# Feature tiles that overlap in the middle instead of doubled last columns, in a fused S5 scan and gated unit

## The chip, the cores and the metric

The kernel runs on one core of a Trainium2 chip. The metric is device time in microseconds of one launch, the median of the runs shown. The core has five engines, each with its own instruction stream that is worked off in order: TensorE (PE; its weight loads are shown apart as PEld), VectorE (DVE), ScalarE (ACT), GpSimd (POOL) and SyncE (SP). SP issues nearly all transfers here, and sixteen DMA engines carry them.

## The reference

x has 2048 tokens of 448 features. It is normalised over the features, and two branches read the result: a diagonal complex recurrence over time (S5), and a gated unit with inner width 1792. The output is `x + s * g`.

```
xn = layernorm(x)
Lam_bar = exp(dt * Lam);  Bu = xn @ B_bar.T          # 448 complex states
h[t] = Lam_bar * h[t-1] + Bu[t]                      # over 2048 tokens
s = 2 * Re(h @ C.T) + xn * Dskip
g = silu((sigmoid(xn @ w_gate) * (xn @ w_up)) @ w_down)
out = x + s * g                                      # bf16
```

## The kernel before

**Chunks.** The tokens are worked in four chunks of 512 (`TC`), each of four tiles of 128. All products with xn sum over features, so xn is turned: `xnT[c]` holds features on the partitions. 448 is three and a half times 128. The turned xn has four tiles: features 0 to 127, 128 to 255, 256 to 383, and a fourth in which features 384 to 447 lie twice, on partitions 0 to 63 and again on 64 to 127. For that the 64 last columns of the normalised xn are copied behind the 448 before the turn (`ln_twice`, and in chunk 0 `ln_turn`), so that a row has 512 columns. Chunk 0 is turned by TensorE through PSUM (`tps`, emptied by `ln_out`), chunks 1 to 3 by DMA transposes on the SP queue, one for each tile of 128 tokens.

**Two halves at a time.** Most products are issued as pairs on 64 partitions: one on the upper, one on the lower half of the array, side by side (`beside_each`, `Sum.add`, line 510). A sum over 448 features is seven such half products. The doubled fourth tile is what lets gate take its last 64 features from the upper half and up from the lower one: the weight rows 384 to 447 of gate and up lie together in `wt`, gate on partitions 0 to 63 and up on 64 to 127, the other rows in `wg` and `wu` as three tiles of 128.

**B and C.** B (448 x 448, real and imaginary) is loaded into `raw["b_re"]` and `raw["b_im"]`, the last columns are doubled (`emit_b_twice`, a memset for the real part), and eight DMA transposes from SBUF write `bT` (`emit_b`, line 297). C is loaded into `c_re` (room `raw_c`) and `c_im` (room `raw_re`, which `b_re` had before), with the doubled columns loaded as small extra DMAs, and is turned by eight DMA transposes (`emit_c_turn`, line 169) into `tc_re` and `tc_im`. Then `emit_c` makes seven scaled tiles `ct`: ScalarE writes a scratch tile, VectorE adds the other part. The scratch tiles take rooms that are free by then; `c_room` lists them, and the first pair lies in `raw_im`, where `b_im` had been.

**The order of the work** is written out: `keep_order` ties each engine's instructions to the written order. SP's order is: x of chunk 0, the weights of the first 512 inner columns, B, the weights of columns 512 to 1023, x of chunk 1, the first block of B turned, the last 768 weight columns around the second turn, Dskip, four more turns of B, x of chunk 2, then (`second_chunk`, and the calls of `at(0, 7, ...)`) two turns of xn, the last block of B, two more turns of xn, w_down, C, and with chunk 1 the turns of C. The tile framework gives each DMA one of eight semaphores in turn, so a DMA can only be issued when the eighth before it has landed.

In a chunk, `emit_line` names the pairs of units: a unit of the gate and up products (`gu_unit`, 128 inner columns) or of B (`bu_unit`, a block of states). For chunk 1 it begins (0, -1), (1, -2), then the down products of chunk 0 (`emit_downs`), then (2, 3), (4, -3), where -1 to -4 are B's blocks. Each product has a PSUM bank, and the eight banks are handed out in turn (`bank`). ScalarE empties the banks of gate, up, B and down; VectorE does the rotation, the scan and the gates. Between them `fill` and `at` place the other work: the first three C scalings stand on ScalarE after the second quarter of chunk 0's down products (`"down1"`).

Of the kernel before, what the change touches and what calls it, by code (L numbers as in the profile page):

```python
# [17 lines left out]
D = 448  # L18
# [9 lines left out]
CP = D // KT  # L28
NT = S_TOK // P
NPK = 2 * D  # L30
EPS = 1e-5
TWO_PI = 2.0 * math.pi
HALF_PI = 0.5 * math.pi
# [30 lines left out]
def kernel(  # L64
# [48 lines left out]
    skip = w.tile([P, D], BF16, name="skip")  # L113


    def load_rows(eng, t, mat, f0, f1):
        eng.dma_start(out=t[:, 0:3, f0:f1], in_=mat[0:384, f0:f1].rearrange("(kt p) f -> p kt f", p=P))
        eng.dma_start(out=t[0:64, 3, f0:f1], in_=mat[384:448, f0:f1])

    def load_w(eng, f0, f1, between=None):  # L120
        for t, mat in ((wg, B_w_gate), (wu, B_w_up)):
            eng.dma_start(out=t[:, :, f0:f1], in_=mat[0:384, f0:f1].rearrange("(kt p) f -> p kt f", p=P))
        if between:
            between()
        for mat, p0 in ((B_w_gate, 0), (B_w_up, 64)):
            eng.dma_start(out=wt[p0:p0 + 64, f0:f1], in_=mat[384:448, f0:f1])

    pool.memset(ident[:], 0.0)
    pool.affine_select(out=ident[:], in_=ident[:], compare_op=ALU.not_equal, fill=1.0, base=0,  # L129
# [126 lines left out]

    def ln_norm(c, j):
        t = c * TPC + j
        xb = xn[c % 3]
        if c < 2:  # L260
            dve.tensor_scalar(out=xb[:, j, 0:D], in0=x_t[c][:, j, :], scalar1=mv[:, t, 0:1],
                              scalar2=rsd[:, t, :], op0=ALU.subtract, op1=ALU.mult)
        else:
            act.activation(xb[:, j, 0:D], x_t[c][:, j, :], ACT.Identity, bias=nmr[:, t, :],
                           scale=rsd[:, t, :])

    def ln_turn(c, j):
        xb, cols = xn[c % 3], slice(j * P, (j + 1) * P)
        if c > 0:
            sync.dma_start_transpose(out=xnT[c][:, 0:KT, cols], in_=xb[:, j, :])  # L270
            return
        (dve if j < 2 else pool).tensor_copy(out=xb[:, j, D:DP], in_=xb[:, j, 384:D])
        for kt in range(KT):
            pe.transpose(tps[j % 2][:, kt, :], xb[:, j, kt * P:(kt + 1) * P], ident[:])  # L274

    def ln_twice(c, copy, j0=0, j1=TPC):
        copy(out=xn[c % 3][:, j0:j1, D:DP], in_=xn[c % 3][:, j0:j1, 384:D])
# [8 lines left out]
    def emit_b_twice():  # L286
        t = raw["b_im"]
        act.copy(out=t[:, 0:3, D:DP], in_=t[:, 0:3, 384:D])
        act.copy(out=t[0:64, 3, D:DP], in_=t[0:64, 3, 384:D])

    def emit_b(cc, pt):
        n = P if pt < 3 else 64
        if cc == 0:
            p0 = pt * P
        else:
            p0 = D if pt == 3 else 512 + pt * P
        sync.dma_start_transpose(out=bT[:, :, p0:p0 + n], in_=raw[("b_re", "b_im")[cc]][0:n, pt, :])

    def bu_cols(pt, cc):
        if pt == 3:  # L300
# [156 lines left out]
    def emit_c(i):  # L457
        pt = i // 2
        tre, tim = ctr["c_re"][:, pt, :], ctr["c_im"][:, pt, :]
        if pt == 3:  # L460
            ta, sa, tb, sb = tre, K["cr3"][:, 0:1], tim, K["nci2"][:, 3:4]
        elif i % 2 == 0:
            ta, sa, tb, sb = tre, K["cr2"][:, pt:pt + 1], tim, K["nci2"][:, pt:pt + 1]
        else:
            ta, sa, tb, sb = tim, K["ncr2"][:, pt:pt + 1], tre, K["nci2"][:, pt:pt + 1]

        if not c_room:
            for nm in ("raw_im", "raw_c"):
                both = []
                c_room.extend((nm, both, k) for k in range(2))  # L470
                if nm == "raw_im":
                    c_room.extend((None, None, None) for _ in range(2))
            c_room.append((None, None, None))
        nm, both, k = c_room[len(mixed)]
        mixed.append(i)
        if nm is None:
            tmp = sp.tile([P, D], FP32, name="c_tmp", tag="ctmp")[:]
        else:
            if k == 0:
                both.append(w.tile([P, 2, D], FP32, name="c_tmps", tag=nm))  # L480
            tmp = both[0][:, k, :]
        act.activation(tmp, tb, ACT.Copy, scale=sb)
        return lambda: dve.scalar_tensor_tensor(out=ct[:, i, :], in0=ta, scalar=sa, in1=tmp, op0=ALU.mult, op1=ALU.add)
# [207 lines left out]

    def gu_halves(c, ft, gt, ut, first, n0=0, n1=TC):
        f0, f1 = ft * P, (ft + 1) * P
        for t, p0 in ((gt, 0), (ut, 64)):
            pe.matmul(t[:, n0:n1], lhsT=wt[p0:p0 + 64, f0:f1],  # L695
                      rhs=xnT[c][p0:p0 + 64, 3, n0:n1], start=first, stop=not first)

    def gu_wholes(c, ft, gt, ut, first, n0=0, n1=TC, which=(0, 1)):
        f0, f1 = ft * P, (ft + 1) * P
        for t, wm in [((gt, wg), (ut, wu))[i] for i in which]:  # L700
            for kt in range(3):
                pe.matmul(t[:, n0:n1], lhsT=wm[:, kt, f0:f1], rhs=xnT[c][:, kt, n0:n1],  # L702
                          start=(first and kt == 0), stop=(not first and kt == 2))


    def gu_out(ft, gt, ub):
# [11 lines left out]
    def gu_unit(c, ft):  # L718
# [70 lines left out]

    def y_ops(c, j, rows, d0=0, d1=D, skipped=False):  # L790
        sl = slice(j * P, (j + 1) * P)
        o = [(ident[rows, :], xn[c % 3][rows, j, d0:d1], d0, d1)] if skipped else []
# [20 lines left out]

    def emit_two(c, j):

        xb, two = xn[c % 3][:, j:TPC:2, 0:D], slice(j, TPC, 2)
# [10 lines left out]

    def emit_rest_of(c, j):
        t = op_.tile([P, D], BF16, name="t_g", tag="zb", bufs=4)
        dve.tensor_tensor(out=t[:], in0=xn[c % 3][:, j, 0:D], in1=gs[c][:, j, :], op=ALU.mult)  # L830
# [64 lines left out]
    def ln_plan(c):  # L895
# [16 lines left out]
        at(own, "down0", 0.0, lambda: ln_twice(c, act.copy))  # L912

    dummy = w.tile([P, 1], FP32, name="dummy")
    act.activation(dummy[:], hpi[:], ACT.Exp)
# [86 lines left out]
    for t in (TPC, TPC + 2):  # L1002
# [13 lines left out]
    def second_chunk(j0):  # L1016
        ln_pow(TPC + j0, 2)
        for j in (j0, j0 + 1):
            ln_norm(1, j)
        ln_twice(1, dve.tensor_copy, j0, j0 + 2)  # L1020
# [4 lines left out]
    at(0, 7, 0.0, lambda: sync.dma_start(out=wd[:], in_=B_w_down.rearrange("(ft p) d -> p ft d", p=P)))  # L1025
    at(0, 7, 0.0, lambda: load_c("c_re", A_C_re, A_C_im))
# [123 lines left out]
```

## Time and profile before

| What | Value |
|---|---|
| median of 3 runs | 184.19 us (184.07 to 184.24) |
| span of the profiled execution | 182.6 us |
| around the span, by the median | 1.6 us |
| PE busy in the span | 177.7 us (97%) |
| DVE busy | 165.0 us (90%) |
| ACT busy | 114.1 us (63%) |
| first weight products on PE | 6.79 us |
| SP issues w_down | 31.66 us |
| down products of chunk 0 on PE | 41.3 to 51.8 us |
| SP issues the eight turns of C | 41.16 to 52.9 us |

The page gives the profiled execution's own time as its span, from the first to the last instruction; the runs' times have 1.6 us more. "Idle before" is the time in which an engine stood still before an instruction, with what ended it. Idle time of an engine that isn't the bottleneck costs nothing by itself. SPq rows are issues of DMAs on the SP queue: their duration is the time that the queue was held, and the data land later. L510 is the line of a helper through which most products go; they are told apart by their tiles.

### The profile page before, as it was taken

How to read it: one execution, taken by the hardware profiler on the slowest of the kernel's cores; microseconds unless marked ns; L12 is line 12 of the kernel's file. 1: busy time of each engine (PE TensorE's matmuls, PEld its weight loads, DVE VectorE, ACT ScalarE, POOL GpSimd, SP SyncE). 2: the span in 40 equal slices, each digit the busy share in tenths (PEclk: the TensorE clock that was granted, in tenths of full speed). 3: DMA queues.
4: the chain of work that ended last, by engine and by line, in shares of the span. 5: the costliest groups of instructions: out<-in, count | busy, mean ns of one | idle time of the engine just before them, and what ended most of it. 6: DMA issues, size and time to landing. Idle time of an engine off the chain costs nothing.

```text
span 182.6 us, 4348 instructions
## 1 busy us (share of the span) xinstructions
PE 177.7 (97%) x1644; PEld 98.3 (54%) x1644; DVE 165.0 (90%) x337; ACT 114.1 (63%) x236; POOL 24.5 (13%) x61
## 2 busy tenths in 40 slices
PE   7999999999999999999999999999999999999992
PEld 7776644446654444645654445545665544645552
DVE  4899999799989979999999999599999999699983
ACT  3999577979487787997367766057048567144100
POOL 4768546321000000004000000000000000000000
PEclk9999999999999999999999999999999999999999
DMA  5999997895434113011251010030001000011112
GB/s 152 312 307 252 231 161 106 229 311 111 104 76 89 29 32 101 4 52 52 41 79 29 4 29 0 4 101 0 4 2 29 4 13 17 4 50 50 29 36 68
DMA packets 27659, 15.07 MB, mean 83 GB/s; under 512 B 16243, under 2 KB 27638, under 8 KB 27638
## 3 DMA queue, kind: packets, MB, share of 16 engines
q1 hardware_dynamic: 27632, 14.79, 35.1%
q8 instruction: 13, 0.21, 0.5%
q14 instruction: 8, 0.07, 0.2%
q10 hardware_dynamic: 6, 0.00, 0.0%
HBM read 8.49 MB, written 1.84 MB: 57 GB/s over the span
## 4 chain that ended last, share of the span: by engine, by line
PE 97%; DVE 1%; POOL 0%; issue 0%; POOLq 0%; DVEq 0%
PE g_ps L510 25%; PE u_ps L510 19%; PE d_ps L510 17%; PE bu L510 12%; PE y_ps L510 11%; PE d_ps L1093 6%; PE warm_ps L192 2%; PE g_ps L702 2%; PE u_ps L702 1%; PE tp_x L274 1%; PE g_ps L695 1%; DVE sg L846 0%; DVE o_l L852 0%; DVE xnT L282 0%; POOL ident L129 0%
## 5 line engine op out<-in xcount | busy, mean ns | idle before, releaser
L510 PE MATMUL u_ps<-xnT,wu 64*128 64x512 bf16 x312 | 68.9, 376 | 0.0
L510 PE MATMUL g_ps<-xnT,wg 64*128 64x512 bf16 x312 | 62.0, 376 | 0.0
L740 ACT ACTIVATE sig<-g_ps 128x512 bf16<-128x512 f32 x52 | 29.1, 597 | 29.1 <-PE g_ps L510 29.1
L510 PE MATMUL bu<-xnT,bT 64*128 64x512 bf16 x196 | 45.7, 376 | 0.0
L510 PEld LDWEIGHTS <-wu 64*128 64x128 bf16 x312 | 25.3, 94 | 17.8 <-POOLq L512 1.6
L510 PE MATMUL d_ps<-wd,hF 64*128 64x448 bf16 x336 | 32.9, 349 | 0.0
L510 PEld LDWEIGHTS <-wg 64*128 64x128 bf16 x312 | 22.7, 94 | 17.6 <-POOLq L512 1.9
L740 ACT CAST ub<-u_ps 128x512 bf16<-128x512 f32 x52 | 29.3, 604 | 0.8 <-DVE hF L712 0.8
L510 PEld LDWEIGHTS <-hF 64*128 64x128 bf16 x336 | 19.9, 94 | 12.1
L510 PEld LDWEIGHTS <-bT 64*128 64x128 bf16 x196 | 17.7, 94 | 10.7
L510 PE MATMUL y_ps<-ct,h 64*128 64x448 bf16 (+2 forms) x203 | 22.7, 343 | 0.0
L589 DVE TENSOR_TENSOR_SCAN wv<-r_col,st,ta 128x512 bf16<-128x512 f32 x18 | 22.6, 1274 | 0.1
L737 DVE TENSOR_TENSOR hF<-sig,ub 128x512 bf16<-128x512 bf16 x52 | 20.9, 416 | 1.3 <-ACT ub L740 1.1
L510 PE MATMUL u_ps<-xnT,wt 64*128 64x512 bf16 x52 | 19.6, 376 | 0.0
L510 PE MATMUL g_ps<-xnT,wt 64*128 64x512 bf16 x52 | 19.6, 376 | 0.0
L510 PEld LDWEIGHTS <-h 64*128 64x128 bf16 (+1 forms) x203 | 13.4, 95 | 8.0
L570 ACT CAST bus<-bu 128x512 bf16<-128x512 f32 x24 | 14.3, 595 | 2.3 <-PE g_ps L510 2.3
L764 ACT ACTIVATE sigd<-d_ps 128x448 bf16<-128x448 f32 x12 | 6.6, 550 | 12.4 <-PE d_ps L510 12.4
L238 POOL TENSOR_TENSOR rsd<-ve,mhalf 128x1 f32<-128x1 f32 (+2 forms) x8 | 7.5, 932 | 48.5 <-PE u_ps L510 45.6
L510 PEld LDWEIGHTS <-wt 64*128 64x128 bf16 x104 | 9.8, 94 | 5.5 <-DMA wt<-in_B_w_up_dram 0.4
L1093 PE MATMUL d_ps<-wd,hF 128*128 128x448 bf16 x56 | 10.9, 353 | 0.0
L819 DVE TENSOR_TENSOR o_t<-y_ps,xn 128x448 bf16<-128x448 f32 x12 | 6.9, 618 | 3.7 <-PE y_ps L510 3.7
(153 smaller groups left out, 229.8 us busy)
## 6 DMA issues: line engine op xcount, KB each, us to landing
wd<-in_B_w_down_dram SPq DMA_DIRECT2D x1, 1568.0 KB, 7.6
x<-in_A_x_dram SPq DMA_DIRECT2D x3, 448.0 KB, 5.5
out_dram<-o_t SPq DMA_DIRECT2D x6, 224.0 KB, 2.1
wg<-in_B_w_gate_dram SPq DMA_DIRECT2D x2, 384.0 KB, 4.4
wu<-in_B_w_up_dram SPq DMA_DIRECT2D x2, 384.0 KB, 5.3
wg<-in_B_w_gate_dram SPq DMA_DIRECT2D x1, 576.0 KB
wu<-in_B_w_up_dram SPq DMA_DIRECT2D x1, 576.0 KB, 8.6
bsw<-bus SPq DMA_DIRECT2D x8, 64.0 KB, 2.0
```

The source lines that it names most:

```text
L192: pe.matmul(warm_ps[:], lhsT=ident[:], rhs=ident[:], start=True, stop=True)
L238: pool.tensor_tensor(out=rsd[:, t:t + n, :], in0=ve[:, t:t + n, :], in1=mhalf[:, 0:n, :], op=ALU.pow)
L274: pe.transpose(tps[j % 2][:, kt, :], xb[:, j, kt * P:(kt + 1) * P], ident[:])
L510: m = pe.matmul(self.t[:, n0:n1], lhsT=lhsT, rhs=rhs, start=self.done == 1, stop=self.done == self.n)
L570: empty = [lambda cc=cc: act.copy(out=bus[:, cc, :], in_=pst[cc][:]) for cc in range(2)]
L589: dve.tensor_tensor_scan(out=T["wv"][:, cc, :], data0=rb, data1=T["ta"][:, cc, :], initial=(0.0 if c == 0 else st[pt][:, cc, :]), op0=mul, ...
L702: pe.matmul(t[:, n0:n1], lhsT=wm[:, kt, f0:f1], rhs=xnT[c][:, kt, n0:n1], start=(first and kt == 0), stop=(not first and kt == 2))
L737: dve.tensor_tensor(out=h[:], in0=sig[:], in1=ub[:], op=ALU.mult)
L740: u.empty = [lambda: act.activation(sig[:], gt[:], ACT.Sigmoid), lambda: act.copy(out=ub[:], in_=ut[:])]
L764: act.activation(sigd[:], ds[j][:], ACT.Sigmoid)
L819: dve.tensor_tensor(out=o[:, i, :], in0=ys[c, j + 2 * i][:], in1=xb[:, i, :], op=ALU.add)
L1093: pe.matmul(ds[j][:], lhsT=hF[c, ft][:, j * P:(j + 1) * P], rhs=wd[:, ft, :], start=ft == 0, stop=ft == FT - 1)
```

## The change

The four feature tiles become 0 to 127, 128 to 255, 192 to 319 and 320 to 447 (`K_ROWS`). The second and third overlap in features 192 to 255, and no tile is doubled. Gate sums tiles 0, 2 and 3 whole and the upper half of tile 1; up sums tiles 0, 1 and 3 whole and the lower half of tile 2. B's sums take their seven halves in the same way.

The weight tiles are laid out to match: `wg` holds rows 0 to 127 and 192 to 447, `wu` rows 0 to 255 and 320 to 447, and `wt` gate's rows 128 to 191 and up's 256 to 319. Each stretch of columns is loaded by six DMAs instead of four.

In chunks 1 to 3 the norm writes all 512 columns itself, as two runs of 256 that both contain features 192 to 255, and the copies go; later readers take xn as two runs of 224. In chunk 0 nothing is doubled, and TensorE turns at the four offsets. B isn't loaded any more: sixteen DMA transposes of 256 columns read it from DRAM. The room `raw_im` is gone with it, and the C scratch tiles and the last rests take `raw_re` and `raw_c` in its place.

```diff
@@ constants
+HD = D // 2
+K_ROWS = (0, 128, 192, 320)
+GATE_K, UP_K = (0, 2, 3), (0, 1, 3)
+def two_runs(ap: bass.AP, step: int, n: int) -> bass.AP:
+    return bass.AP(tensor=ap.tensor, offset=ap.offset, ap=[*ap.ap[:-1], [step, 2], [1, n]])
@@ weights and B
-    def load_w(eng, f0, f1, between=None):
-        for t, mat in ((wg, B_w_gate), (wu, B_w_up)):
-            eng.dma_start(out=t[:, :, f0:f1], in_=mat[0:384, f0:f1].rearrange("(kt p) f -> p kt f", p=P))
...
+    def load_w(eng, f0, f1):
+        def rows(mat, r0, r1):
+            m = mat[r0:r1, f0:f1]
+            return m.rearrange("(kt p) f -> p kt f", p=P) if r1 - r0 > P else m
+
+        eng.dma_start(out=wg[:, 1:3, f0:f1], in_=rows(B_w_gate, 192, 448))
+        eng.dma_start(out=wg[:, 0, f0:f1], in_=rows(B_w_gate, 0, 128))
+        eng.dma_start(out=wu[:, 0:2, f0:f1], in_=rows(B_w_up, 0, 256))
+        eng.dma_start(out=wu[:, 2, f0:f1], in_=rows(B_w_up, 320, 448))
+        eng.dma_start(out=wt[0:64, f0:f1], in_=rows(B_w_gate, 128, 192))
+        eng.dma_start(out=wt[64:128, f0:f1], in_=rows(B_w_up, 256, 320))
...
-    for nm, mat in (("b_re", A_B_re), ("b_im", A_B_im)):
-        raw[nm] = w.tile([P, KT, DP], BF16, name=nm, tag="raw" + nm[1:])
-        load_rows(sync, raw[nm], mat, 0, D)
-    dve.memset(raw["b_re"][:, :, D:DP], 0.0)
@@ norm and turn of xn
+        xb, src = xn[c % 3][:, j, :], x_t[c][:, j, :]
+        if c == 0:
+            xb = xb[:, 0:D]
+        else:
+            xb, src = two_runs(xb, 2 * P, 2 * P), two_runs(src, 192, 2 * P)
...
+    def xn_runs(c, j):
+        return two_runs(xn[c % 3][:, j, :], HD if c == 0 else DP - HD, HD)
...
-        (dve if j < 2 else pool).tensor_copy(out=xb[:, j, D:DP], in_=xb[:, j, 384:D])
         for kt in range(KT):
-            pe.transpose(tps[j % 2][:, kt, :], xb[:, j, kt * P:(kt + 1) * P], ident[:])
-
-    def ln_twice(c, copy, j0=0, j1=TPC):
-        copy(out=xn[c % 3][:, j0:j1, D:DP], in_=xn[c % 3][:, j0:j1, 384:D])
-        for j in range(j0, j1):
-            ln_turn(c, j)
+            pe.transpose(tps[j % 2][:, kt, :], xb[:, j, K_ROWS[kt]:K_ROWS[kt] + P], ident[:])
@@ turn of B
-    def emit_b(cc, pt):
+    def emit_b(pt):
         n = P if pt < 3 else 64
...
-        sync.dma_start_transpose(out=bT[:, :, p0:p0 + n], in_=raw[("b_re", "b_im")[cc]][0:n, pt, :])
+        for cc, mat in enumerate((A_B_re, A_B_im)):
+            p0 = bu_cols(pt, cc)[0] + cc * (64 if pt == 3 else 0)
+            for kt in (0, 2):
+                sync.dma_start_transpose(out=bT[:, kt:kt + 2, p0:p0 + n],
+                                         in_=mat[pt * P:pt * P + n, K_ROWS[kt]:K_ROWS[kt] + 2 * P])
@@ skip and the rooms of the C scratch tiles
-        t = xn[c % 3][:, :, 0:D]
-        dve.tensor_tensor(out=t, in0=t, in1=bcast_mid(skip[:], TPC), op=ALU.mult)
+        t = xn_runs(c, slice(0, TPC))
+        by = two_runs(skip[:], HD, HD).unsqueeze(1).to_broadcast((P, TPC, 2, HD))
+        dve.tensor_tensor(out=t, in0=t, in1=by, op=ALU.mult)
...
-            for nm in ("raw_im", "raw_c"):
+            for nm in ("raw_re", "raw_c"):
                 both = []
                 c_room.extend((nm, both, k) for k in range(2))
-                if nm == "raw_im":
+                if nm == "raw_re":
                     c_room.extend((None, None, None) for _ in range(2))
@@ products (gu_halves and gu_wholes likewise)
-                    for kt in range(n)]
+                    for kt in (range(KT) if n == KT else (UP_K, GATE_K)[h])]
...
-            o = [(sums[i], ((wg, wu)[i][HALF[h], kt, f], x[HALF[h], kt, :], 0, TC)) for kt in range(3)]
-            return o + [(sums[i], (wt[HALF[h], f], x[HALF[h], 3, :], 0, TC))] * tail
+            o = [(sums[i], ((wg, wu)[i][HALF[h], k, f], x[HALF[h], kt, :], 0, TC))
+                 for k, kt in enumerate((GATE_K, UP_K)[i])]
+            return o + [(sums[i], (wt[HALF[h], f], x[HALF[h], 1 + i, :], 0, TC))] * tail
@@ output
-            dve.tensor_tensor(out=o[:, i, :], in0=ys[c, j + 2 * i][:], in1=xb[:, i, :], op=ALU.add)
+            dve.tensor_tensor(out=two_runs(o[:, i, :], HD, HD), in0=two_runs(ys[c, j + 2 * i][:], HD, HD),
+                              in1=xn_runs(c, j + 2 * i), op=ALU.add)
...
-            room_of_rests.append(w.tile([P, 2, D], FP32, name="t_x", tag=("raw_re", "raw_im")[j // 2]))
+            room_of_rests.append(w.tile([P, 2, D], FP32, name="t_x", tag=("raw_re", "raw_c")[j // 2]))
@@ the written order
-        if pt == 0:
-            emit_b_twice()
...
-    emit_b(0, 0)
-    load_w(sync, 1024, F, lambda: emit_b(1, 0))
+    emit_b(0)
+    load_w(sync, 1024, F)
     sync.dma_start(out=skip[:], in_=A_Dskip.partition_broadcast(P))
-    for pt in range(1, KT - 1):
-        for cc in range(2):
-            emit_b(cc, pt)
+    emit_b(1)
+    emit_b(2)
     load_x(2)
...
-    at(0, 7, 0.0, lambda: [emit_b(cc, KT - 1) for cc in range(2)])
+    at(0, 7, 0.0, lambda: emit_b(KT - 1))
```

More of the change, by code (lines that the diff above doesn't have):

```diff
@@ L258, in ln_norm @@
         t = c * TPC + j
-        xb = xn[c % 3]
+        xb, src = xn[c % 3][:, j, :], x_t[c][:, j, :]
[3 more added lines that the diff above has]
+            xb, src = two_runs(xb, 2 * P, 2 * P), two_runs(src, 192, 2 * P)
         if c < 2:
-            dve.tensor_scalar(out=xb[:, j, 0:D], in0=x_t[c][:, j, :], scalar1=mv[:, t, 0:1],
-                              scalar2=rsd[:, t, :], op0=ALU.subtract, op1=ALU.mult)
-        else:
-            act.activation(xb[:, j, 0:D], x_t[c][:, j, :], ACT.Identity, bias=nmr[:, t, :],
-                           scale=rsd[:, t, :])
+            dve.tensor_scalar(out=xb, in0=src, scalar1=mv[:, t, 0:1], scalar2=rsd[:, t, :], op0=ALU.subtract,
+                              op1=ALU.mult)
+        else:
+            act.activation(xb, src, ACT.Identity, bias=nmr[:, t, :], scale=rsd[:, t, :])
+    def xn_runs(c, j):
+        return two_runs(xn[c % 3][:, j, :], HD if c == 0 else DP - HD, HD)
     def ln_turn(c, j):
@@ L693, in gu_halves @@
         f0, f1 = ft * P, (ft + 1) * P
-        for t, p0 in ((gt, 0), (ut, 64)):
+        for t, p0, kt in ((gt, 0, 1), (ut, 64, 2)):
             pe.matmul(t[:, n0:n1], lhsT=wt[p0:p0 + 64, f0:f1],
-                      rhs=xnT[c][p0:p0 + 64, 3, n0:n1], start=first, stop=not first)
+                      rhs=xnT[c][p0:p0 + 64, kt, n0:n1], start=first, stop=not first)
     def gu_wholes(c, ft, gt, ut, first, n0=0, n1=TC, which=(0, 1)):
         f0, f1 = ft * P, (ft + 1) * P
[L700 to L703, printed above, removed]
+        for t, wm, kts in [((gt, wg, GATE_K), (ut, wu, UP_K))[i] for i in which]:
+            for k, kt in enumerate(kts):
+                pe.matmul(t[:, n0:n1], lhsT=wm[:, k, f0:f1], rhs=xnT[c][:, kt, n0:n1],
+                          start=(first and k == 0), stop=(not first and k == 2))
     def gu_out(ft, gt, ub):
@@ L791, in y_ops @@
         sl = slice(j * P, (j + 1) * P)
-        o = [(ident[rows, :], xn[c % 3][rows, j, d0:d1], d0, d1)] if skipped else []
+        o = [(ident[rows, :], xn_runs(c, j)[rows, d // HD, :], d, d + HD) for d in range(d0, d1, HD)] if skipped else []
         for pt in range(3):
@@ L829, in emit_rest_of @@
         t = op_.tile([P, D], BF16, name="t_g", tag="zb", bufs=4)
-        dve.tensor_tensor(out=t[:], in0=xn[c % 3][:, j, 0:D], in1=gs[c][:, j, :], op=ALU.mult)
+        dve.tensor_tensor(out=two_runs(t[:], HD, HD), in0=xn_runs(c, j), in1=two_runs(gs[c][:, j, :], HD, HD),
+                          op=ALU.mult)
         if j % 2 == 0:
-            room_of_rests.append(w.tile([P, 2, D], FP32, name="t_x", tag=("raw_re", "raw_im")[j // 2]))
+            room_of_rests.append(w.tile([P, 2, D], FP32, name="t_x", tag=("raw_re", "raw_c")[j // 2]))
         rests[j] = room_of_rests[j // 2][:, j % 2, :]
@@ L911, in ln_plan @@
             at(own, "down0", 0.0, lambda j=j: ln_norm(c, j))
-        at(own, "down0", 0.0, lambda: ln_twice(c, act.copy))
+        at(own, "down0", 0.0, lambda: [ln_turn(c, j) for j in range(TPC)])
     dummy = w.tile([P, 1], FP32, name="dummy")
@@ L1019, in second_chunk @@
             ln_norm(1, j)
-        ln_twice(1, dve.tensor_copy, j0, j0 + 2)
+        for j in (j0, j0 + 1):
+            ln_turn(1, j)
     at(0, 7, 1.0, lambda: second_chunk(0))
-    at(0, 7, 0.0, lambda: [emit_b(cc, KT - 1) for cc in range(2)])
+    at(0, 7, 0.0, lambda: emit_b(KT - 1))
     at(0, 7, 1.0, lambda: second_chunk(2))
```

17 lines of the change are left out of this document (1 added, 16 removed).

## The prediction

> **What bounds the kernel now.** I read the page's shares and its chain, then the waits, then the SP queue, ScalarE and TensorE in order of time over the first 60 us, which is where every edit that is not a reshaped access pattern lies.
>
> ```profile
> PE 177.7 (97%) x1644; PEld 98.3 (54%) x1644; DVE 165.0 (90%) x337; ACT 114.1 (63%) x236; POOL 24.5 (13%) x61
> PE 97%; DVE 1%; POOL 0%; issue 0%; POOLq 0%; DVEq 0%
> ACT c_tmps L482 <- DMA tc_re<-c_re: 2.6, 1, 2.6
> DVE ct L483 <- DMA tc_im<-c_im: 0.8, 1, 0.8
> PEld L510 <- DMA wt<-in_B_w_up_dram: 0.4, 1, 0.4
> ```
>
> TensorE is the bound nearly everywhere: the change can win only some tenths (its idle time), and whatever makes TensorE wait is added in full. Of the waits (total, times, longest), 0.4 us at 21.9 us is a weight tile that landed late, and 2.6 us is ScalarE waiting for the turned C. The SP queue (start, duration):
>
> ```profile
> 9.86 1.29 SPq L297 DMA_TRANSPOSE bT<-b_re  x1
> 11.20 0.57 SPq L122 DMA_DIRECT2D wg<-in_B_w_gate_dram  x1
> 12.40 1.91 SPq L297 DMA_TRANSPOSE bT<-b_im  x1
> ...
> 25.90 1.79 SPq L297 DMA_TRANSPOSE bT<-b_re  x1
> 27.79 1.19 SPq L297 DMA_TRANSPOSE bT<-b_im  x1
> ...
> 31.66 0.57 SPq L1025 DMA_DIRECT2D wd<-in_B_w_down_dram  x1
> ...
> 41.16 5.78 SPq L169 DMA_TRANSPOSE tc_re<-c_re  x4
> 47.04 5.86 SPq L169 DMA_TRANSPOSE tc_im<-c_im  x4
> ```
>
> The reader is to see one in-order line: B's turns, the late weights, w_down, C's loads, C's eight turns. And the engines that live on its end:
>
> ```profile
> 45.23 0.40 ACT L277 COPY xn<-xn 128x256 bf16<-128x256 bf16 x1
> 48.22 1.23 ACT L482 ACTIVATE c_tmps<-tc_re,nci 128x448 f32<-128x448 bf16 x2 [2.58 <-DMA tc_re<-c_re]
> ...
> 49.91 0.52 ACT L764 ACTIVATE sigd<-d_ps 128x448 bf16<-128x448 f32 x1
> ...
> 53.30 0.55 ACT L766 CAST zb<-d_ps 128x448 bf16<-128x448 f32 x1
> 54.19 1.28 DVE L483 SCALAR_TENSOR_TENSOR ct<-tc_im,ncr,c_tmps 128x448 bf16<-128x448 bf16 x2 [0.84 <-DMA tc_im<-c_im]
> 55.48 0.38 PE L510 MATMUL bu<-xnT,bT 64*128 64x512 bf16 x1
> ```
>
> ScalarE starts its first C scaling when c_re is turned (48.22), VectorE its first ct when c_im is turned (54.19): six microseconds lie between the two.
>
> **The change, part by part. The room of the C scalings** is the edit that I expect to decide. The scratch tile of the first two scalings takes the room of raw_im before, which only B used and which is free by 30 us. Now it takes raw_re, where c_im lies until its four turns have read it; the built order of the changed kernel has the first scaling wait on all eight DMA semaphores, the four turns of c_im included. So ScalarE can't start it at 48.22 but only when the last c_im turn has landed, at 54.1 by the ct that waited for the same turn (issued at 51.62, 2.4 to landing). ScalarE is in order. Behind the scaling stand two more, then the four pairs sigd and zb that empty the d_ps banks, then all gate and up evictions. In the profile this row of work runs from 48.22 to 53.85, 5.63 us with 0.29 of waiting in it: 5.34 of work. It would end at 54.2 + 5.34 = 59.5. Who waits: PSUM has eight banks in turn; d_ps take four, units 2 and 3 the other four, and the pair of unit 4 and bu takes d_ps's again. Its fourth pair of products, at 55.48, needs the bank emptied last. So TensorE stands about 59.5 - 55.5 = 4.0, with a semaphore's tenth 4.1 us, if the c_im turns land as before. VectorE, which needs zb for its gates, shifts with it: its stretch from the gates at 52.67 to the tb at 56.59 contains the 0.84 wait, which goes, so it ends no later against TensorE than now. Nothing later gives this back, since TensorE has no idle time to shrink.
>
> **When the c_im turns land.** They follow w_down and C's loads on one queue, so they move with w_down's issue, 31.66. From 9.86 (x of chunk 1 stays the 16th DMA: four more weight DMAs, four B loads fewer) SP has eight B turns before: 1.29+1.91+1.20+2.24+1.27+1.27+1.79+1.19 = 12.16 us. Afterwards it has sixteen of half the columns, from DRAM, at s each, two more weight loads at 0.57, and ten more gaps of 0.06: w_down at 31.66 - 12.16 + 16s + 1.7 = 21.2 + 16s. No row shows a turn from DRAM. Lower end: the fastest plain DMA, 0.37. Upper end: the turns from SBUF, 1.19 to 1.29 whether 64 or 128 rows. Plain loads there take 0.57; if the 0.68 that a turn takes beyond it went by blocks of 128 columns, half would be 0.91. I take 0.65, nearer to the plain load, since the source is DRAM like a load's: w_down at 31.6, no shift. Each 0.1 is 1.6 us. A floor holds below: xn of chunk 1 is written by VectorE from 22.2, so the queue can't go on before 22.6, and then come four turns of xn (5.1) and four of B: 22.6 + 5.1 + 4(s+0.06) = 30.1 at s of 0.5, 1.6 earlier than now.
>
> [...]
>
> **The packets of these turns.** A 128x512 turn shows 512 packets of 256 bytes, about 20 ns each on 16 engines, 0.64 us of all of them. From DRAM I have no row: 0.3 us per half turn at that rate, 0.8 at the 51 ns of an 896-byte load packet. I take 0.4. Against it the B loads go, 0.8 MB at 308 GB/s, 2.6 us out of a stretch in which the engines are full from 4 to 22 us. At 0.8 the second B block lands near 25.5 and is read at 26.4: still covered.
>
> **Weights.** Before the first products the same bytes come in four DMAs instead of two; the engines still have a backlog (wu landed at 7.55, issued by 3.1), so one microsecond of later issue is hidden by it; without that cover up to 1.0 us. The late ones have 2.6 us less ahead of them, so the 0.43 us wait at 21.9 goes.
>
> **Chunk 0 and 1 without copies.** Two copies on VectorE (0.18, 0.21) and two on POOL (0.23, 0.24) go; the fourth turn of each tile on TensorE waited for them. At most 0.2 at 6.8 us and 0.25 at 9.4. With the 0.43 this is up to 0.9 us of TensorE, but it is lost again at 55 us, where the end of the SP line decides, so I count it at nothing; it would be kept only if that wait were short. For chunk 1 four norms at 0.39 grow to 0.45 and two copies of 0.20 go, 0.2 saved beside TensorE; for chunks 2 and 3 four ScalarE norms at 0.77 grow to 0.88 and a copy of 0.40 goes: even. B's copies (0.35 and 0.24 on ScalarE) and a memset (0.17) were beside TensorE too.
>
> **Reshaped patterns.** The skip product, o_t and the last rests read two runs of 224 instead of one of 448, same elements. The skip product takes 1.08 us for 1792 elements, 0.60 ns each; if it fell to the 1.38 ns of o_t (0.618 for 448) it would be 2.47, four times 1.4 = 5.6 us on VectorE, which has 17.6 idle. I take no change, since they stay runs of 448 bytes. TensorE's list of products is the same row for row.
>
> **The sum.** Span 182.6; the rows' time is the span, and 184.19 - 182.6 = 1.6 us lies around it in the runs shown, which I leave as it is. 184.19 + 4.1 + 0 = 188.3 us.
>
> **The rivals.** (a) *The turns from DRAM hold SP as long as those from SBUF*, s near 1.25 (for it: the time did not fall with half the rows; against: another source, half the blocks). w_down at 41.2, 9.5 later, C's turns with it: 4.1 + 9.5, about 198. From s of 0.9 on, 192. (b) *The queue runs at its floor*, and C's turns without the 1.9 and 2.0 us issues in their row: landing at 51.2 to 52.5, a wait of 1.2 to 2.5, 185.4 to 186.7. For it: 2.6 us less traffic; against: C's first turn waited for its load, landed at 41.1, and behind it 1.57 MB of w_down. (c) *Faster*: the wait never reaches TensorE. The chain of ScalarE would have to end by 55.5 less the 0.9 gained, so c_im's last turn must land by 49.2, 4.9 earlier than now; the floor gives 1.6, and 1.3 more without the slow issues. Then 183.5. Only a much faster load of w_down and C would do it. (d) That the change does not do what it says: the added wait is in the built program, so this can only be its length.
>
> **How the numbers follow.** The likeliest, s from 0.5 to 0.9, 186.7 to 192: 0.65. (a) and s over 0.9: 0.18. (b): 0.11. (c): 0.04. Within 0.2% (0.4 us, about what a measurement of this kernel can tell from no change): 0.02, between (b) and (c). The range takes in (b)'s upper half and the likeliest with the lower part of (a): 185.8 to 194.5. Slower by over 0.2%: 0.94.
>
> **What would show it.** Right: ScalarE idle for 7 to 9 us before its first c_tmps, released by a turn of tc_im; TensorE idle some 4 us near 55 us; the sixteen B turns at 0.5 to 0.9 each on SP; the 0.4 us wait for wt gone; no other wait of TensorE over 0.5. Wrong: B turns at 1.2 each, TensorE waiting already for bT or xnT before 36 us; or C's turns landed before 50 us; or VectorE's skip product near 2.5 us.

## The result, and the profile after

| | before | after |
|---|---|---|
| median of 4 runs each, same chip | 184.22 us (184.07 to 184.53) | 199.66 us (198.84 to 200.89) |
| ratio | 1 | 1.083, 95% interval 1.079 to 1.088 |
| span of the profiled execution | 182.6 us | 198.3 us |
| mean granted TensorE clock | 1.000 | 0.974 |
| SP issues w_down | 31.66 us | 41.74 us |
| first down product on TensorE | 41.0 us | 49.6 us |
| last c_im turn has landed | 54.1 us | 64.7 us |

The change costs 15.4 us. The forecast of 188.3 us and its range up to 194.5 were too low. Medians are of all runs of a kernel; the ratios, here and below, leave out single executions over 1.5% above the fastest of their kernel (one each of e6, e7, e8 and e10). The page of after, its busy shares and the shares of its chain:

```profile
PE 183.2 (92%) x1644; PEld 99.1 (50%) x1644; DVE 165.2 (83%) x332; ACT 113.3 (57%) x232; POOL 23.6 (12%) x59
...
PE 65%; SPq 20%; DMA 7%; ACT 4%; issue 2%; DVE 1%; ACTq 0%; DVEq 0%
```

Before, TensorE was 97% of the chain. Now a fifth of it is the SP queue itself: time in which the queue was issuing a transfer and the rest waited for its place in line. VectorE's work is the same (165.2 against 165.0 us). The SP queue in order (start, duration; x2 is two turns):

```profile
9.29 2.56 SPq L294 DMA_TRANSPOSE bT<-in_A_B_re_dram  x2
11.89 4.16 SPq L294 DMA_TRANSPOSE bT<-in_A_B_im_dram  x2
16.09 0.58 SPq L128 DMA_DIRECT2D wg<-in_B_w_gate_dram  x1
...
25.10 3.00 SPq L294 DMA_TRANSPOSE bT<-in_A_B_re_dram  x2
...
33.99 2.52 SPq L294 DMA_TRANSPOSE bT<-in_A_B_re_dram  x2
36.55 2.51 SPq L294 DMA_TRANSPOSE bT<-in_A_B_im_dram  x2
39.16 2.53 SPq L279 DMA_TRANSPOSE xnT<-xn  x2
41.74 0.57 SPq L1025 DMA_DIRECT2D wd<-in_B_w_down_dram  x1
...
57.53 5.95 SPq L172 DMA_TRANSPOSE tc_im<-c_im  x4
```

B's sixteen turns hold SP for 22.3 us, a single one for 1.24 us at the median, 64 rows (33.99, 36.55) as long as 128, and a turn of xn, 128x512 from SBUF, is no longer (39.16). So sixteen turns hold the queue for 22.3 us where the eight before held it for 12.2, and w_down goes out 10.1 us later. The waits of after (total, times, longest):

```profile
ACT c_tmps L481 <- DMA tc_im<-c_im: 11.5, 1, 11.5
PE g_ps L509 <- ACT zb L766: 4.2, 1, 4.2
PE bu L509 <- DMA bT<-in_A_B_im_dram: 3.0, 4, 1.5
PEld L509 <- DMA wu<-in_B_w_up_dram: 2.1, 2, 1.6
```

None of these four stood before. The first two belong to the shared room, the last two to the late queue. The 11.5 us of the first contain some of the late queue too: with a room of its own (e1, below) the same scaling still waits 7.43 us. TensorE in order of time, at its two worst places:

```profile
30.82 0.38 PE L509 MATMUL u_ps<-xnT,wu 64*128 64x512 bf16 x1
32.65 0.60 PE L509 MATMUL bu<-xnT,bT 64*128 64x512 bf16 x1 [1.46 <-DMA bT<-in_A_B_im_dram]
33.05 0.63 PE L509 MATMUL bu<-xnT,bT 64*128 64x512 bf16 x1
...
63.02 0.38 PE L509 MATMUL u_ps<-xnT,wt 64*128 64x512 bf16 x1
67.61 0.58 PE L509 MATMUL g_ps<-xnT,wg 64*128 64x512 bf16 x1 [4.21 <-ACT zb L766]
68.47 0.58 PE L509 MATMUL bu<-xnT,bT 64*128 64x512 bf16 x1 [0.29 <-ACT zb L766]
```

At 32.65 TensorE waits for a block of B, at 67.61 for the bank that ScalarE empties after its late scalings. Behind each pause a product takes 0.58 to 0.63 us instead of 0.38, and the pairs follow each other every 0.43 us instead of 0.215. The table by stretch of after gives the reason (start:end, length, PE, PEld, DVE, ACT, POOL busy, granted clock, DMA share, GB/s):

```profile
30.00:32.00 2.00, 0.61 (x4) 0.11 (x4) 2.00 (x4) 0.00 (x0) 0.00 (x0) 0.98 0.24 40
32.00:34.00 2.00, 1.35 (x8) 0.54 (x10) 0.95 (x4) 0.00 (x0) 0.39 (x3) 0.50 0.82 214
34.00:36.00 2.00, 2.00 (x16) 0.79 (x14) 0.81 (x2) 1.18 (x3) 0.16 (x1) 0.66 0.85 164
36.00:38.00 2.00, 2.00 (x22) 0.88 (x20) 0.96 (x2) 1.97 (x5) 0.25 (x2) 1.00 0.11 20
...
66.00:68.00 2.00, 0.39 (x1) 0.10 (x1) 0.39 (x1) 2.00 (x6) 0.00 (x0) 0.52 0.62 126
70.00:72.00 2.00, 2.00 (x11) 0.79 (x11) 1.97 (x6) 2.00 (x5) 0.00 (x0) 0.50 0.00 0
72.00:74.00 2.00, 2.00 (x18) 0.94 (x16) 1.97 (x5) 1.11 (x4) 0.00 (x0) 0.78 0.00 0
```

The clock was at 0.50 when work came back after each pause, and was full again by 35.4 and 72.9 us. A full stretch at half clock has 11 products (70 to 72) where one at full clock has 22 (36 to 38), both with PE "2.00 busy": the busy column alone hides it. Six pairs at 0.43 instead of 0.215 are 1.3 us at each of the two places (32.65 to 35.2, and 70.2 to 72.7, where ScalarE no longer set the pace). Products at half clock count as longer busy ones, so the busy PE row grows (183.2 us against 177.7) for the same 1644 products.

### The profile page after: what moved, and what is told of

Same layout as the page of the kernel before. It is cut to its first block, busy times and chain, and to the rows that moved or that the text cites. A ratio compares the mean times of both kernels' runs of the same rounds, so it can differ in the third digit from the quotient of the medians.

```text
span 198.3 us, 4353 instructions
## 1 busy us (share of the span) xinstructions
PE 183.2 (92%) x1644; PEld 99.1 (50%) x1644; DVE 165.2 (83%) x332; ACT 113.3 (57%) x232; POOL 23.6 (12%) x59
## 4 chain that ended last, share of the span: by engine, by line
PE 65%; SPq 20%; DMA 7%; ACT 4%; issue 2%; DVE 1%; ACTq 0%; DVEq 0%
PE g_ps L509 17%; PE u_ps L509 13%; PE d_ps L509 11%; PE y_ps L509 10%; PE bu L509 8%; SPq L294 8%; PE d_ps L1093 5%; SPq L172 5%; DMA c_re<-in_A_C_im_dram 4%; DMA bT<-in_A_B_im_dram 2%; DMA tc_im<-c_im 1%; SPq L133 1%; SPq L128 1%; SPq L132 1%; SPq L131 1%
## 5 line engine op out<-in xcount | busy, mean ns | idle before, releaser
L509 PE MATMUL u_ps<-xnT,wu 64*128 64x512 bf16 x312 | 69.6, 380 | 1.1 <-DMA wu<-in_B_w_up_dram 1.1
L509 PE MATMUL g_ps<-xnT,wg 64*128 64x512 bf16 x312 | 63.3, 384 | 4.9 <-ACT zb L766 4.2
L509 PE MATMUL bu<-xnT,bT 64*128 64x512 bf16 x196 | 50.3, 398 | 3.7 <-DMA bT<-in_A_B_im_dram 3.0
L509 PEld LDWEIGHTS <-wg 64*128 64x128 bf16 x312 | 22.4, 95 | 18.8 <-issue 2.5
L588 DVE TENSOR_TENSOR_SCAN wv<-r_col,st,ta 128x512 bf16<-128x512 f32 x18 | 22.6, 1275 | 0.1
L509 PE MATMUL g_ps<-xnT,wt 64*128 64x512 bf16 x52 | 20.1, 386 | 0.0
L769 DVE TENSOR_TENSOR g_t<-zb,sigd 128x448 bf16<-128x448 bf16 x12 | 4.2, 385 | 7.9 <-ACT zb L766 7.9
```

The costliest lines, as they stand in the source:

```text
L509: m = pe.matmul(self.t[:, n0:n1], lhsT=lhsT, rhs=rhs, start=self.done == 1, stop=self.done == self.n)
L588: dve.tensor_tensor_scan(out=T["wv"][:, cc, :], data0=rb, data1=T["ta"][:, cc, :], initial=(0.0 if c == 0 else st[pt][:, cc, :]), op0=mul, ...
L769: dve.tensor_tensor(out=gs[c][:, j, :], in0=zb[:], in1=sigd[:], op=ALU.mult)
```

## The experiments

The two suspects are separate edits, so the room was undone alone in the changed kernel (e1), and each was put alone into the kernel before (e4, e6). The other runs ask what is left of the tiles when both are gone.

**e1: own room, the late queue left.** In the changed kernel the C scratch tiles take `raw_im` again, which nothing else uses.

```diff
-            for nm in ("raw_re", "raw_c"):
+            for nm in ("raw_im", "raw_c"):
...
-                if nm == "raw_re":
+                if nm == "raw_im":
```

> The changed kernel, but the first two C scalings take a room of their own (raw_im) again. Theory (a turn holds the SP queue 1.24 us whatever its size, and the shared room makes ScalarE wait for the last turn of c_im, not of c_re): ScalarE's first c_tmps is released by tc_re, which landed at 60.24 in the changed kernel, so its row of 5.34 us ends at 65.7 instead of 70.2, and 4.5 us of the 15.4 lost come back: 195.1 us (194.3 to 195.8). Rival (all of the loss comes from B's turns being late, and the room costs nothing beside it): 199 us as now.

Measured: 194.2 us, ratio 1.052 (1.048 to 1.056), 0.1 us below the expected range. ScalarE's row of e1:

```profile
60.77 1.23 ACT L481 ACTIVATE c_tmps<-tc_re,nci 128x448 f32<-128x448 bf16 x2 [7.43 <-DMA tc_re<-c_re]
```

The scaling is released by a turn of c_re, not c_im, and TensorE's 4.2 us pause is gone: beside zb only 0.49 us waits, twice, are left, and the clock stays at 1.00 there. So the room costs 5.5 us on top of the late queue, and the late queue 9.8 us. In the profiled execution, whose span is 10.2 us longer than before, 8.7 us of this have come together by the first down product of chunk 0, which starts at 49.73 us and started at 41.00 (the table ahead has 41.3). So most of the late queue's price is paid before C's turns matter: TensorE waits for weights and for blocks of B, and the granted clock is 0.92 over 30 to 34 us and 0.65 over 34 to 38.

**e4: the shared room alone.** The kernel before with the same two lines changed the other way.

```diff
-            for nm in ("raw_im", "raw_c"):
+            for nm in ("raw_re", "raw_c"):
...
-                if nm == "raw_im":
+                if nm == "raw_re":
```

> The kernel before with one line changed: the first two C scalings take raw_re, where c_im lies. Theory: ScalarE's first c_tmps starts at 54.2 instead of 48.2, its row ends at 59.5, TensorE stands from 55.5 to 59.6: 188.3 us (187.8 to 189.0; more if the granted clock falls in the pause, as it did in the changed kernel's pauses). Rival (the banks are free in time, or VectorE's wait there hides it): 184.2 to 185 us.

Measured: 190.14 us, ratio 1.031 (1.027 to 1.035), +5.7 us, above the expected range, which left the clock out. TensorE of e4, and its table by stretch:

```profile
54.27 0.38 PE L510 MATMUL u_ps<-xnT,wu 64*128 64x512 bf16 x1
57.23 0.37 PE L510 MATMUL g_ps<-xnT,wg 64*128 64x512 bf16 x1 [2.58 <-ACT zb L766]
58.10 0.37 PE L510 MATMUL bu<-xnT,bT 64*128 64x512 bf16 x1 [0.49 <-ACT zb L766]
...
59.83 0.58 PE L510 MATMUL u_ps<-xnT,wu 64*128 64x512 bf16 x1 [0.49 <-ACT zb L766]
```

```profile
56.00:58.00 2.00, 0.37 (x1) 0.09 (x1) 0.39 (x1) 2.00 (x6) 0.00 (x0) 1.00 0.54 109
58.00:60.00 2.00, 1.36 (x9) 0.53 (x10) 1.92 (x5) 2.00 (x6) 0.00 (x0) 0.80 0.33 66
60.00:62.00 2.00, 2.00 (x12) 0.78 (x10) 1.93 (x5) 1.73 (x4) 0.00 (x0) 0.50 0.00 0
62.00:64.00 2.00, 2.00 (x19) 0.93 (x16) 2.00 (x5) 1.38 (x3) 0.00 (x0) 0.84 0.00 0
```

Here the predicted mechanism stands alone, at the predicted place. The pair with the first u_ps of unit 4 (59.83), which waits for the last bank, stood at 55.69 before: 4.1 us, the predicted pause. The rest is the half clock: from 59.83 to 62.35 the pairs come every 0.42 us, and the next whole unit starts at 63.35 where it started at 57.63, 5.7 us later. That this is the clock comes from the rows; no run held the clock up across the pause. The two causes add up: 9.8 us (e1) and 5.7 us (e4) are 15.5, and the change cost 15.4.

**e6: sixteen turns alone, from SBUF.** The kernel before, B still loaded, each of its turns split into two of 256 columns.

```diff
-        sync.dma_start_transpose(out=bT[:, :, p0:p0 + n], in_=raw[("b_re", "b_im")[cc]][0:n, pt, :])
+        for kt in (0, 2):
+            sync.dma_start_transpose(out=bT[:, kt:kt + 2, p0:p0 + n],
+                                     in_=raw[("b_re", "b_im")[cc]][0:n, pt, kt * P:(kt + 2) * P])
```

> The kernel before with each of B's eight turns from SBUF split into two of 256 columns; B is still loaded, the tiles stay doubled, the C scalings keep their own room. Theory (SP is held some 1.25 us by each turn, whatever source and size): w_down is issued 8 to 10 us later, near 40 to 41, and the kernel loses what the changed kernel with its own room loses, with B's blocks, the turned xn and w_down late in turn: 193.5 us (191.5 to 195.5). Rival (a half turn holds SP half as long, and only DRAM as source makes it long): 184.4 to 185.5 us.

Measured: 192.7 us, ratio 1.043 (1.038 to 1.047), some 8 us, as expected. The SP queue of e6:

```profile
19.23 2.47 SPq L298 DMA_TRANSPOSE bT<-b_re  x2
21.75 2.53 SPq L298 DMA_TRANSPOSE bT<-b_im  x2
...
40.94 0.57 SPq L1027 DMA_DIRECT2D wd<-in_B_w_down_dram  x1
```

Half the columns from SBUF hold the queue just as long as the whole did, and w_down is 9.3 us late (10.1 in the changed kernel). So it is the number of turns, and neither DRAM nor the size: DRAM or SBUF, 256 or 512 columns, 64 or 128 rows, most of them take 1.2 to 1.3 us.

**e2: six turns from DRAM.** If a turn costs the same whatever its size, larger ones are free. Here one turn takes 448 or 384 rows of B, and all six stand where the first block of B stood, ahead of the late weights; the room stays shared.

```diff
-    def emit_b(pt):
-        n = P if pt < 3 else 64
-        for cc, mat in enumerate((A_B_re, A_B_im)):
+    def emit_b_all():
+        for mat, r0, r1, p0 in ((A_B_re, 0, 448, 0), (A_B_im, 0, 384, 512), (A_B_im, 384, 448, 448)):
             for kt in (0, 2):
-                sync.dma_start_transpose(out=bT[:, kt:kt + 2, p0:p0 + n],
-                                         in_=mat[pt * P:pt * P + n, K_ROWS[kt]:K_ROWS[kt] + 2 * P])
+                sync.dma_start_transpose(out=bT[:, kt:kt + 2, p0:p0 + r1 - r0],
+                                         in_=mat[r0:r1, K_ROWS[kt]:K_ROWS[kt] + 2 * P])
...
-    emit_b(0)
+    emit_b_all()
     load_w(sync, 1024, F)
...
```

> The changed kernel with B turned by six DMA transposes from DRAM (up to 448 rows by 256 columns each) instead of sixteen of at most 128 rows, all issued where the first block's four were. Same bytes, same source, room still shared. Theory (a fixed hold for each turn): 6 x 1.24 = 7.4 us of SP instead of 19.8, w_down is issued near 29 to 31 us instead of 41.7, c_im is turned by about 53, the shared room costs 1 to 3 us, and the late weights still cost the 2 us near 21: 186.5 us (185 to 189). Rival (the hold goes by bytes, or DRAM as the source makes it long): each 448-row turn holds SP for some 4 us, the queue is as late as now, 198 to 200 us.

Measured: 191.57 us, ratio 1.039 (1.035 to 1.042): 5 us above the expected 186.5. The six turns held SP for 9.9 us, more than the expected 7.4 but far from the 22.3 of sixteen: the two 448-row ones for the real part 3.81 us, the four for the imaginary part 6.11. w_down went out at 28.98. But the six weight loads behind the turns went out only from 19.28 on. TensorE of e2:

```profile
23.51 0.39 PE L507 MATMUL g_ps<-xnT,wg 64*128 64x512 bf16 x1 [2.74 <-DMA wg<-in_B_w_gate_dram]
25.29 0.60 PE L507 MATMUL u_ps<-xnT,wu 64*128 64x512 bf16 x1 [0.87 <-DMA wt<-in_B_w_gate_dram]
```

Behind these two waits the pairs come every 0.42 us until 30.8, where 0.215 was usual, which is another 2.7 us; the mean granted clock of this execution is 0.982. TensorE never waits for a `zb` in this kernel, so the shared room cost nothing beside the late weights. The queue is worked off in order, so its lateness moved to what stood behind the turns.

**e3: the six turns behind the late weights, and an own room.** The room's two lines are those of e1.

```diff
-    emit_b_all()
     load_w(sync, 1024, F)
+    emit_b_all()
```

> As the six turns, but the last weight columns are issued ahead of B's turns, and the C scalings have a room of their own. Theory: SP is nowhere late any more, weights land by 17, B by 20, the 0.43 us wait of the kernel before at 21.9 is gone and the two waits for doubled columns too: 183.3 us (182.8 to 184.3), a little faster than before. If B's packets are slow, B lands after 20 us and TensorE waits there 1 to 2 us: 185. Rival (hold by bytes): 196 us or more.

Measured: 185.58 us (10 runs), ratio 1.006 (1.004 to 1.009), above the expected 182.8 to 184.3. With both causes gone, 14.1 of the 15.4 us are gone. The first products come 0.16 us earlier than before and those with `wt` 0.36 us earlier, but TensorE now waits for the imaginary part of B:

```profile
21.66 0.39 PE L507 MATMUL bu<-xnT,bT 64*128 64x512 bf16 x1 [0.44 <-DMA bT<-in_A_B_im_dram]
22.81 0.39 PE L507 MATMUL bu<-xnT,bT 64*128 64x512 bf16 x1 [0.55 <-DMA bT<-in_A_B_im_dram]
```

**e5: e3 with ScalarE issuing the two `wt` loads of the first 512 columns, and the last two weight loads behind B's first four turns.**

```diff
-    load_w(sync, 0, 512)
+    load_w(sync, 0, 512, 0, 4)
...
+    load_w(act, 0, 512, 4, 6)
...
-    load_w(sync, 1024, F)
-    emit_b_all()
+    load_w(sync, 1024, F, 0, 4)
+    emit_b_all((0, 1))
+    load_w(sync, 1024, F, 4, 6)
+    emit_b_all((2,))
```

> The kernel of e3 (six turns, own room) with two more moves on the queues: the two wt loads of the first weight columns are issued by ScalarE, and the late wt loads come behind B's first four turns instead of ahead of them. Theory: SP reaches B's turns 1.2 + 1.1 us earlier than in e3, where their last ones landed some 1.5 us after TensorE could have read them; that wait goes, and what stays is the gain of the copies (about 0.3 us by 9.3 us) and of the weight wait of the kernel before (0.43): 183.8 us (183.2 to 184.6), with the kernel before at 184.4. Rival (the DMA engines, not the queue, set when B lands): as e3, 185.4 to 185.8.

Measured: 185.25 us (12 runs), ratio 1.004 (1.002 to 1.005), between the expected range and the rival's. The wait for B is gone, and two others came in the profiled execution, which is the longest of the twelve (185.73 us). TensorE of e5, then POOL of e5:

```profile
6.98 1.16 PE L698 MATMUL g_ps<-xnT,wg 128*128 128x256 bf16 x9 [0.56 <-DMA wg<-in_B_w_gate_dram]
...
26.32 0.39 PE L506 MATMUL g_ps<-xnT,wg 64*128 64x512 bf16 x1 [0.97 <-POOLq L508]
```

```profile
23.39 0.24 POOL L362 TENSOR_TENSOR den<-t,t 128x4 f32<-128x4 f32 x1
23.72 2.49 POOL L363 TENSOR_SCALAR t<-den 128x4 f32<-128x4 f32 x1
```

The first weights land later, and at 26.3 TensorE waits for POOL's queue, where an empty instruction (`pool.nop` in `Sum.add`) orders a sum's products on one half of the array behind those on the other; an operation on four elements of each partition stood there for 2.49 us.

**e7: e5 with those `wt` loads on SP again.**

```diff
-    load_w(sync, 0, 512, 0, 4)
+    load_w(sync, 0, 512)
...
-    load_w(act, 0, 512, 4, 6)
```

> The kernel of e5 with the two wt loads of the first 512 columns back on SP. If the earlier first products (0.16 us) and weight-tail products (0.36 us) of e3 are kept, and the B wait stays away as in e5, then nothing is left of e3's loss (1.2 us) but the TensorE gap on POOL's queue that e5 showed at 25 us (1.35 us), which e3 did not have: 183.4 to 184.2 us without it, 184.8 to 185.3 us with it. Rival: e3's and e5's loss was not these waits but something spread out (TensorE slower on the overlapping tiles): 185.2 us or more with no wait over 0.5 us in the trace.

Measured: 185.87 us, ratio 1.008 (1.005 to 1.011). The wait on POOL's queue went and the time did not: the two weight loads, put behind four turns, went out at 19.66 and 20.30 and were late. TensorE of e7:

```profile
23.17 0.39 PE L506 MATMUL u_ps<-xnT,wt 64*128 64x512 bf16 x1 [0.89 <-DMA wt<-in_B_w_up_dram]
```

So the expected 183.4 to 184.2 did not come. The rival's number did, 185.2 or more, but not for the rival's reason, which was a loss without any wait over 0.5 us: there is one of 0.89.

**e8: the change with only B's path put back.** B is loaded as two runs of columns (six loads instead of four, since the runs overlap), and eight turns from SBUF go where they stood before; the room is `raw_im`.

```diff
+    for nm, mat in (("b_re", A_B_re), ("b_im", A_B_im)):
+        raw[nm] = w.tile([P, KT, DP], BF16, name=nm, tag="raw" + nm[1:])
+        for r in (0, 1):
+            sync.dma_start(out=raw[nm][:, 0:3, 2 * P * r:2 * P * (r + 1)],
+                           in_=mat[0:384, 192 * r:192 * r + 2 * P].rearrange("(kt p) f -> p kt f", p=P))
+        sync.dma_start(out=raw[nm][0:64, 3, :].rearrange("p (r f) -> p r f", r=2),
+                       in_=two_runs(mat[384:D, :], 192, 2 * P))
     load_w(sync, 512, 1024)
...
```

> The changed kernel with only its B path put back: B is loaded again (as two runs of 256 columns, so that it lies like the overlapping tiles and nothing is doubled), and eight turns of 512 columns from SBUF go where they stood before; the C scalings have raw_im again. Everything else of the change stays (tiles, six weight loads for each stretch, norms of 512 columns, no copies). If the loss is the number of turns on SP and the shared room and nothing else, w_down goes out within 2 us of 31.7, no wait of TensorE over 0.6 us, and the time is 183.5 to 184.6 us. Rival: the overlapping tiles or the six weight loads cost something of their own, as the 0.4 to 0.8% of the six-turn kernels could also be read: 185.0 to 186.0 us.

Measured: 188.03 us (186.09 to 189.73), ratio 1.014 (1.008 to 1.019), above the expected range and the rival's. TensorE of e8, in an execution of 188.85 us:

```profile
15.75 0.82 PE L515 MATMUL g_ps<-xnT,wg 64*128 64x512 bf16 x6 [1.62 <-DMA wg<-in_B_w_gate_dram]
16.98 0.39 PE L515 MATMUL g_ps<-xnT,wt 64*128 64x512 bf16 x1 [0.41 <-DMA wt<-in_B_w_gate_dram]
```

Weights again: the second stretch goes out at 9.05 instead of 6.76, behind two more weight loads and two more loads of B, and w_down at 35.48.

**e9: e8 with that stretch of weights ahead of B's loads.**

```diff
+    load_w(sync, 512, 1024)
     for nm, mat in (("b_re", A_B_re), ("b_im", A_B_im)):
...
-    load_w(sync, 512, 1024)
```

> The kernel of e8 with the weights of columns 512 to 1023 issued ahead of B's six loads. In e8 TensorE stood 1.6 and 0.4 us at 14 to 17 us for these weights, which went out 2.3 us later than before. If e8's loss is that, those gaps go; the late weights still go out 3 to 4 us later than before, so up to 1.5 us of waiting at 22 to 25 us remains: 184.5 to 186.0 us. Rival: the overlapping tiles cost TensorE something elsewhere: 187 us or more.

Measured: 189.07 us (186.7 to 189.13), ratio 1.020 (1.013 to 1.027). The gaps at 14 to 17 us went, as expected, and the time is above the expected 186.0. It is in the rival's range, but the rival had the overlapping tiles slow TensorE elsewhere, and the rows show late weights. TensorE of e9, then its table by stretch:

```profile
21.19 0.39 PE L515 MATMUL g_ps<-xnT,wg 64*128 64x512 bf16 x1 [0.57 <-DMA wg<-in_B_w_gate_dram]
24.47 0.60 PE L515 MATMUL u_ps<-xnT,wu 64*128 64x512 bf16 x1 [2.46 <-DMA wu<-in_B_w_up_dram]
```

```profile
22.00:24.00 2.00, 0.01 (x2) 0.00 (x0) 2.00 (x7) 0.58 (x1) 1.21 (x1) 0.99 1.06 290
24.00:26.00 2.00, 1.53 (x8) 0.45 (x10) 1.34 (x5) 0.00 (x0) 0.00 (x0) 0.50 1.62 120
26.00:28.00 2.00, 2.00 (x14) 0.74 (x12) 0.00 (x0) 0.39 (x1) 0.99 (x5) 0.65 0.64 138
```

The late weights, issued 5 to 7 us later than before, cost 3.0 us of waiting where I expected up to 1.5, and some 1.4 us of half clock behind it. No other wait of TensorE behind the first products is listed for this kernel.

**e10: six weight loads for each stretch, alone.** The kernel before, each load of 384 weight rows split in two.

```diff
-            eng.dma_start(out=t[:, :, f0:f1], in_=mat[0:384, f0:f1].rearrange("(kt p) f -> p kt f", p=P))
+            eng.dma_start(out=t[:, 0:2, f0:f1], in_=mat[0:256, f0:f1].rearrange("(kt p) f -> p kt f", p=P))
+            eng.dma_start(out=t[:, 2, f0:f1], in_=mat[256:384, f0:f1])
```

> The kernel before with each load of 384 weight rows split into two, of 256 and 128 rows, so that each stretch of columns is loaded by six DMAs as in the change; nothing else differs. If the count of loads is what is left of the change's loss, each stretch takes some 1.0 us more of SP's queue, the last weights go out some 3 us later, and the 0.4 us wait for wt at 21.9 us grows to 1 to 2.5 us: 184.8 to 186.5 us. Rival: the backlog of the DMA engines hides the later issue, as I had counted it: 184.0 to 184.6 us.

Measured: 186.58 us (10 runs, 184.99 to 188.18), ratio 1.009 (1.006 to 1.012), at the upper end of what was expected. TensorE of e10, in an execution of 187.41 us:

```profile
15.29 0.39 PE L511 MATMUL g_ps<-xnT,wt 64*128 64x512 bf16 x1 [0.61 <-DMA wt<-in_B_w_gate_dram]
...
56.86 0.37 PE L511 MATMUL bu<-xnT,bT 64*128 64x512 bf16 x1 [0.49 <-ACT zb L767]
58.59 0.37 PE L511 MATMUL u_ps<-xnT,wu 64*128 64x512 bf16 x1 [0.49 <-ACT zb L767]
```

The same bytes in two more issues for each stretch, some 0.5 us of queue each, cost this kernel 0.9%: once through a weight tile at 15 us, and once through C's turns, which begin at 44.99 instead of 41.16. The wait that was expected to grow, for wt at 21.9 us, did not: it is 0.44 at 22.4. So the six loads that the change makes of four have a price, which the prediction had at nothing. That they are the whole of what is left in e3, e5, e7, e8 and e9 is not shown. None of these beats the kernel before.

## Why the prediction was wrong

**The step that failed is the turns of B, "I take 0.65, nearer to the plain load, since the source is DRAM like a load's".** A turn holds SP for 1.24 us from DRAM. The bounds were right (0.37 to 1.29) and the truth lay at the upper one. The sum for w_down, 21.2 + 16s, gives 41.0 with 1.24, and it went out at 41.74. The row that should have decided was in the trace: 64-row and 128-row turns took the same, so the time did not go with the data. I read it as a point for rival (a), gave that 0.18, and then chose by the source. Two of the signs that the prediction gave for being wrong are there, turns of B at 1.2 us each and TensorE waiting for bT before 36 us. Rival (a), "about 198", was the right case; e6 shows that the hold is the same with SBUF as the source (pairs of turns at 2.47 to 2.58 us, two longer), and e1 gives the late queue's price: 9.8 us. That rival (a)'s 9.5 us come so near is partly luck: it put them at C's turns, near 55 us, and 8.7 us were lost before the first down product, to weights, to B and to the clock. Most plain loads held SP for 0.4 to 0.6 us; how fast the data of a turn move was not tested.

**The room: mechanism right, size off.** ScalarE waited for the last c_im turn, its row of work ran from 64.92 to 70.16, 5.24 us (predicted 5.34), and TensorE stood for the last bank. I had 4.1 us; the runs show 5.5 (after against e1) and 5.7 (e4). The term that was missing is the clock, which no step of the prediction contained: in e4 the pause itself is 4.1 and the half clock behind it 1.6. In after the clock was at 0.50 for 3.41 us at the first place (31.93 to 35.35) and for 6.83 at the second (66.07 to 72.89), where the first products came singly; in e4 it was 0.80, 0.50 and 0.84 in the three stretches from 58 to 64 us, which is some 3.4 us at 0.50. TensorE had not stood still all the time ahead of the fall: of the 3.41 us before it, it was busy for 1.64 and 0.74 us in after, and for some 1.4 in e4. What makes the clock fall was not tested.

**Packets.** They did not matter: between 24 and 28 us, with B's turns back to back, the DMA engines were at a share of 0.25. The queue, not the data, set the pace.

**Weights.** "The 0.43 us wait at 21.9 goes" was wrong. In the kernel before those 0.43 us were idle time of the weight loads, and the products came only 0.1 us late there (21.85 after 21.54, where pairs take 0.215). In after a wait of 1.15 us for wu and 0.23 for wt stand at 22 to 23, since the weights went out behind four turns at 16.09 instead of from 11.20 on. That the first weights' later issue is hidden was right (first products at 6.58 in after against 6.79). That the extra loads cost nothing otherwise is not so: e10 lost 0.9%.

**Copies, reshaped patterns.** The copies' gain exists, 0.16 and 0.36 us in e3, and counting it at nothing was right, but it is lost to waits at 22 us and not at 55. The skip product takes 1.084 us in both kernels at the median: runs of 224 cost nothing.

**The floor.** The sum for the earliest w_down, "22.6 + 5.1 + 4(s+0.06) = 30.1 at s of 0.5", gives 29.9. With turns of 1.24 us the floor was never reached, so nothing hangs on it.

**What stays open.** The five kernels with both causes removed stand 0.4 to 2.0% above the kernel before, each with other waits of TensorE on weights, on B or on POOL's queue, read in one execution each. That the tiles would gain if these could all be avoided is not shown.

## What to carry to other kernels

Price a queue by the number of its issues, not by their bytes: a turn held SP for 1.24 us at half the columns too, so that sixteen took 22.3 us of the queue where eight took 12.2, and the bill came far away, at what stood behind it in line. When a duration in the trace does not change with the size, expect the fixed part to be all of it over the sizes seen, and let that row outweigh a plausible story on the source. When an edit frees a buffer, look who takes its place in the remaining ones, and where TensorE will stand, count what the clock may take behind the pause: 1.3 to 1.6 us for each 3.41 us at 0.50 here.

## What the runs showed of the hardware

- Most DMA transposes held the SP queue for 1.19 to 1.3 us whether they turned 64x256, 128x256 or 128x512, from DRAM or from SBUF (before, after; pairs of 2.47 to 2.58 in e6), and two of 384x256 took 2.61 together (e5, e7). The pairs with 448x256 took 3.81 (e2), 4.19 (e3), 4.59 (e5) and 4.99 (e7), all between 9 and 17.2 us; 128x512 turns took up to 2.24 in the first 30 us before. What lengthens single ones was not isolated.
- TensorE's granted clock in after was 0.50 from 31.93 to 35.35 (3.41 us) and from 66.07 to 72.89 (6.83, twice that), and 1.00 otherwise until the work ended; 30.72 us, nine times 3.41, lie between the two. The tables by stretch come to 3.44 us at 0.50 in e4 (from 59.2), e1 (from 33.4) and e9 (from 24.0), if the clock was 1.00 or 0.50 there too, and the mean of e2's execution, 0.982 over 189.4 us, to 6.8. The length of one pause does not sort them: in e4 the clock stayed at 1.00 for 2.0 us behind the pause of 2.58, and in e1 it fell though no wait of TensorE behind its first products is listed that was longer than 1.1 us.
- In after it fell behind the two 3.41 us with the least work of TensorE, busy for 1.64 us (28.52 to 31.93) and for 0.74 (62.66 to 66.07); in the other stretches of that length at 1.00, from 4.63 us until the work ended, it was busy for 2.57 us or more. Half rate ended behind 3.41 us with 2.70 us of work (31.93 to 35.35) and went on behind 1.59 (66.07 to 69.48). What decides it was not tested.
- In e5 a POOL operation on four elements of each partition took 2.49 us while VectorE worked without a break beside it; the two before it and the two behind it took 0.2 to 0.6. TensorE waited 0.97 us for the empty instruction behind it in POOL's queue.
